# Dividing attention by its sums on GpSimd, in the layout in which it is summed

## The chip, the cores and the metric

The kernel runs on one core of a Trainium2 chip, as one launch. The metric is the time on the device in microseconds, the median of several runs. The engines are called by their short names: PE (TensorE: matmuls, with PEld for its weight loads), DVE (VectorE), ACT (ScalarE), POOL (GpSimd) and SP (SyncE, which here issues DMAs).

## The reference

One conformer block over 2 x 4000 tokens of 144 features, 4 heads of 36, in bfloat16:

```
h = silu(layernorm(x) @ w_ff1a) @ w_ff1b;      x = x + 0.5 * h
q, k, v = split(layernorm(x) @ w_qkv)          # 4 heads of 36
p = softmax(q @ k.T * 36 ** -0.5);             x = x + (p @ v) @ w_o
a, b = split(layernorm(x) @ w_pw1)
c = depthwise_conv5(a * sigmoid(b), dw);       x = x + silu(c) @ w_pw2
h = silu(layernorm(x) @ w_ff2a) @ w_ff2b;      x = x + 0.5 * h
out = layernorm(x)
```

Attention is over all 4000 keys of a sequence, for each of its 4000 queries.

## The kernel before

**Tiles.** The 8000 tokens are 16 chunks of 500 (`CH`), eight to a sequence; a chunk is 4 blocks of 125 tokens. For a chunk of queries attention runs over 62 tiles of 64 keys and a rest of 32, 1008 tiles in all. A tile's scores for the four heads are four 64x64 matmuls, in two banks of PSUM with 128 rows (two heads) by 1000 columns. Then comes the exponential, by one of the ways in the table `TYPES`:

- 'A': ACT does it in one instruction (PT<-PS, 128x1000); 'R' is the same for the rest.
- 'D': DVE does it in five: two passes from PSUM to integers (one for each bank, 128x500), then on the tile in SBUF "y" and "w" (TENSOR_SCALAR on 16-bit integers, 128x1000) and "m" (TENSOR_TENSOR). 'W' is the same with one pass over both banks (128x1000). The sums of these tiles take twice the matmuls.

Four or eight matmuls (PS<-PT,VA) add the tile to two PSUM banks `BX` and `BX+1`: by column, the 500 queries; by row, 36 features of one head and, in row 36, the sum of the exponentials; from row 64 on, the next head. This is the column layout: features down the partitions, tokens along the columns.

**The end of a chunk.** `epilogue` copies the two banks to SBUF as f32 (`OTF`, 128x1000, laid over columns of the queries QT that are no longer read; DVE COPY QT<-PS). PE transposes it, eight f32 matmuls against an identity (PS<-IDF,QT), into two banks with tokens down the partitions. There the sum is a column: for each bank DVE takes the reciprocal (RD<-PS) and multiplies (AN<-PS,RD, 125x288). `post1` transposes the result AN back with one DMA on SP (XTB<-AN); only the last chunk does it with PE. The output projection is eight matmuls of 72 rows (PS<-WO,XTB), added to x by `residual`. Then the chunk's layer norm, GLU, convolution and second feed-forward follow.

**Layer norms.** DVE takes statistics, POOL a power and the normalisation XN<-X,RS, block by block, and a DMA on SP transposes XN. Some of these, and copies and residual additions, can be done by another engine; a letter for each in the table `UNITS` says which ('d' DVE, 'a' ACT, 'p' POOL). A residual on ACT adds x on PE, with two further matmuls against EYE or IDENT.

**Order.** A planner in Python (`Rec`, `Sched`) writes down the instructions with costs and dependences. The tables then fix what runs: `ORDER` the order on each engine, `TYPES` the exponentials, `BANKS` and `SLOTS` the places of the attention tiles, `PLACES` other banks, `UNITS` the engines. Each engine runs its list in order, with waits on semaphores only where a dependence needs one. The first chunks' feed-forward and projections come ahead of any exponential; afterwards the other work of the block runs between the tiles; after the last exponential the tail holds what is left of the last chunks. All instructions are issued from one helper (L588 to L595), so groups in the profile are told apart by tiles and shapes.

Of the kernel before, what the change touches and what calls it, by code (L numbers as in the profile page):

```python
# [13 lines left out]
H = 4  # L14
# [26 lines left out]
        '+9+&+##.+[+Z+T+O+E+_+`+R+S+J+I+K+2+8+U+c+d+k+3+H+h+g+6+7+N+r+q#/+v+u+l+i+b+^+f+z+y+a,&+]+}+j,!+s+t+w'
        '+X,++e+x,%#0,1,0+{+Y,*,$+o+p,4,5#1,8,9+V#2,=,<,),2+m+W,G,#,7,F,A,@+n,:,3,6,K,J,(+|,>,;,/,,,N,O,H,S,I'
        ',.,R,-,?,Z#3,W,V,L,Q,M,P,b,a#4,f,e,[,X,U,T,Y,i,j#5,m,n,d,B,q,C,x,w#6,{,|,g,l,c,r-#-$#7-)-(,h,k,z-,,p'
        '-2-3,o#8-6-7,y-+-*,E-%-&-;-:,}-!,^,_,]---?->#9-C-B,u-K-<-9-=-8-F-G-4,`,D-1-P-Q,t-.,v-@-5-J-U-T-D-E-X'
        '-I-0-/-_-`-Y-A-H,s-d-c#<-g-h#:#;#>#?#=-k-l-o-b-p-e-f-w-j-N-W-i-V-O-t-s#@#A#B-x-a.!-}#C.&.%-L-S-R-M.*'
        '.+./-q-r.#-u-v...$#D#E.8.9-^.-.,.).<.=-]#F.@.A.;.3.:-m-n.D.E.0#G.1-{.I.H.2-z.>.?.(.L.M-|.P.Q-Z.K.B.^'
        '._-y.O.F-[.T.C.N.J.G.b.c.7.R.S.X.f.6.5.g.j.V.U.4.k.W#H#I.a.h.u.t.`.y.x.e.d.n.|.}#J.o.l.m.z/%.i/$.{/)'
        '/-/#.[/*.Z/!.v.].Y.w/4/3#K/7/8/./+/,/(/</;#L/@/?#M/I/C/J.p/6/5/:/9/N/M.s.q/A/D.r/&/B#N/Q/R/L///U/P/_'
        '/=/V/K#O/Z/Y/2/^/1/>#P/d/m/n/O/0/W/F/[/H/r/q#Q/u/v/h/E/G/c/]/g0$0#/T/S/a/b/`/X0(0)/y/f/e0302#R07060,'
        '0%0;/s0:0&04/p/o050+0-0E0D0*/t/z/w09080H0I0=0</x0>/k0L0M0F/l#S0P0Q#T0U0T/j/i0G0?/}0Y0X0K0N#U0d0c0!0R'  # L50
        '0]0S0J0g0h/|0l/{0Z0[0k0O#V0o0p000/0j0i010e0s0t0.0^0f0V0w0x#X#W0{0W0|0B0C0m1#0v0n0y1$0u#Y1.1/0q0z1!1('
        '0}0b1213#Z161710111)0r0a1:1;#[1>1?#]1B1C1%0A#^1&1J0@1A1G1F1P1Q151<0`181K0_1@191U1T#_#`1I1R1Y1D1X1W1H'
        '1]1M1O1V1^1L1*1S1a1-1N1g1h1b1=141l1k#a1v1u1o1[1,1+1z1y#b2!1}1p1e1i1x1E2-2,2%1`1{1|1_21202$1w1Z1f2#2&'
        '2425#c2>232?1m1j282C2/2B1n1c1q1d#d2F29222G1s1r2Q2P2E2*2+2@262K2A2D2J2U2T2)2.2H1t2X2Y2I#e2(2^2W2]2b2['
        '2a2;2:#f272e2`2S2l2f2<2V2m2N#g2i2r3#2R2s2g2=2w2L2v2M2_2Z2h2c2O3!2d2{2z2k2j3)3*#i3-3.#j2p2q3132#h3536'
        '2y3+3/2x3:393B3A302n342|3=3>372}332o3G383H#k3K3L3,3S3?3%2u3O3P3$3;3T2t3@3I3Z3Y3F3N3M3&3<3_3^3f#l3J3C'
        '3c3[3b3g3m3l3(3Q3a3D3`3R3x3W3X3p3q#m3u3t3]3d3E4(3e3n3j3o3r4#3V4!3U3s4&473y#n#o4-4.3h3i4$3k4%414B4A3v'
        '483w4>4=#p#q#r4I4J4E4F4D4)424/4?40#s4+4,4M4N#t#u4Q4@4C4R4G4L4H4;4V4U4*4O#w#v4a4`3}4K4P494Y4e4d4:#x4h'
        '4i4<3|4T4S4Z4W4s4r454X4m4f4g3z4w4v4l4643444b3{4{4z#y#z5#4t5!5-4u4j5.4}4y4[4x4k4c4|5&52515(4]5$4q4p55'
        '56#{5=5%595:4_4o4^5D5C5>5350574n545/5X5W5<5G5+585N5M#|5F5`5;5H5Q5,5Y5Z5[5]5E5B5O5*5a5)#}5A5P5d5e5^5_'  # L60
        '5?5R5@5i5h$!5m5l$#5q5p5t5f5g6!5}5j5J5b5c5k5I5w6&6%5L5r5o5s5K5x5n5V5U6*6+5T5S5u5v$$6/6.6962$%686(636<'
        '6=$&$(6A6@6$6#6)$)6:6E6?6D656I666;6H$*61606S6R6,6C6L675z6B6W6V$+646M6F5|6Z6G6>6[6e6Y6U5{6f6X6_6-6T6K'
        '$,$-6j6i6^6m6g6]6n6N6O6J6h5y6`6P6w6x$.6q6p6{6Q6o6|6k6l6y6r7#7$$/7(7)$0$17-7,6}6b706d767!7%77$26a717&'
        '7.7;7:6v6u7>7E6z787/7D$37H7I7*7?797<7+6c7M7L$47Q7P7G7F6s6t7T7U$5$674757X7Y7]7S$77d7c7C7J7B7^7g7K7V7h'
        '7R7O7N737q7=7k7r$87v7u7f7i7j727e7l7z7y$97@7W8(8)7}7A7s7b7Z7[8,8-$:81807t7w8!7_7`8*8584$;8?8>83827p88'
        '7|7a8+8B8C7{$<8.8/8F8G8@89867x$=878J8K8D8A7o8&8N8E8H8U8T$>8X8Y7m8$8%8O8L8M8]8^$?8#8W7n8V8g8h8;8a8:8['
        '8Z8I8k8l$@8p8o8`8i8R8b8P8j8s8t$A8x8w8r8q$B8{9)9*8u8=8n9-8Q8<8y9.9!8v8S8m8|8}92918c8d8e8f8_8z96959#$C'
        '9?9@909/9C9D9,99$D9H9G94939:97989+9R9Q$E9F9&9U9V9B9E9K9(9Z9Y$F9_9^9S9L9J9A9$9c9b9%9I9f9]9T9[9l9m$G9p'
        '9q9=9e$H9t9u9X9W9g9`9a9d:#9O:!9>9;9<9r9x9o:(:&$I:,9M9y:$9N:+9P9n:5:6:/:%9j9s9k:::99v:0:.$J:=:*:>:-:B'
        ':)9h:A9}$K:L:E:K9z9{:?:8:7:@:4:O:C:P:3:F9i:<:;:T:S:M:D9w:W:^:_$L:2:X:b:c:U:R:V:G:a:f:N:g:1:H:`:j9|:q'  # L70
        ':p$M:k:I:u:t:d:J:[:e:s:|:i:x:y:r:];&;($N$O;-;.:Y:Z:}:Q;2;1$P;<;;:m:h:{;?;0:n:l;@;/;3:o;4;C;D;5:v;=$Q'
        ';*:z;M;N:w;A;+;B;R;G;Q;%;E;6;$;V;U;);F;H;>;Z;Y$R$S;P;,;W;^;X;_;[;b;O;S;c;7;T$T;];8;f;m;9;#;l;I;L;!;J'
        ';q;K;p;g;e;d$U;t;u;`;o;s;n;x;y$V;|;};r;a<)<$<%$W<,;k;j<-;z;:<7<6;{<2<3;v$X$Y<A<@<*<+<;<:<D<E<#<!;h<('
        '<&;w<H<I;i$Z<M<L$[$]$^$_$`<P<Q<T<C<4<U<?<8<5<B<K<J<N<O<0<9<X<Y<.<1<></<G<]<a<^$a<g<h<S<Z<b<V<F<[<l<k'
        '$b<`<_<v<u<W<o$c<y<z<n<m<R<j<p<<=!<}$d=%=&$e<c<d=*=+<w<{<|=$=2=/=.=)=#<i=3<x=8=9=(=-$f=<==<==L$g=A=@'
        '$h$i$j=E=:=D=?=;=6=1=>=5=4=I<s=M=H<e=7<t<f=,=S=R=B=c=G=F=C=V=W$k=[=Z<q=d=U=J=K=T=_=`$l=i=j=X=Y=^=y<r'
        '=0=m=n$m=q=r=]=z=Q=P=k=l=u=v$n>$>#=s=t=N=O>)>($p$o>,>-=a=}=h>%>1>:>&>0=f=x=w=b=e>7>6=g=p>A>*>/>@$q=o'
        '>!>E>D>;$r>H>I>C=|>B={>+>M>L$t>.>9>P>Q$s>[>Z$u>`>_>U>N>4>5>8>S>c>d>T>K>?>R>J>3>g>h$w$v>l>F>k>G>^>o>='
        '>]>u>v>>>b>a>j>e>f>O>z>y$x>p>m>}><?!>x>i>2>|?&>w>W?%>n>X$y$z?#?2?*?+?(>{?$${?.>Y?7$|?8>s?>?=?,?-?)?1'
        '>r>V?A?B>q>t?0?/?F?E?I?P?O?T?C?D?S$}?W?X?J?6?5?@???V?G?c?b?[?R?Q?g?f%!?Y?k?j?H?d?]?U?<?9?:?;?e?n?Z?t'  # L80
        '?u%#%$?x?y?l?m?o?|?}?h%%@$@%%&?w?z@*?v@)?{@-?i@3?a@4@&%(?M@.?`?N@8@7?3@,@<@+?4@!@A@B@;@#@6?_@5@E@F?^'
# [2417 lines left out]
```

## Time and profile before

| what | value |
|---|---|
| time, median of 3 runs | 868.47 us (868.26 to 868.83) |
| span of the profiled execution | 866.2 us, 27018 instructions |
| granted TensorE clock, mean | 0.999 |
| busy: PE, DVE, ACT, POOL | 98%, 96%, 96%, 33% of the span |
| exponentials on ACT | 777, mean 1080 ns |
| f32 transposes on PE | 128, in groups of four |
| DMA | 26.92 MB, mean 31 GB/s |

The page shows one execution. It gives that execution's span, from the first to the last instruction, and no other time of it; the runs' median is 2.3 us above the span. Busy time counts an engine while at least one of its instructions is under way, and successive instructions overlap at their ends, so durations of a group add up to more than the engine's busy time.

### The profile page before, as it was taken

To read this page: it belongs to the slowest core of one execution; us is meant where nothing else is said; L and a number is where in the kernel's file an instruction comes from. 1 tells how busy PE (TensorE), PEld (TensorE's weight loads), DVE (VectorE), ACT (ScalarE), POOL (GpSimd) and SP (SyncE) were. 2 spreads that over 40 slices of the span, in tenths; PEclk is the share of its full clock that TensorE was granted. 3 is DMA by queue.
4 is the path that set the end of the run, shared out by engine and by line. 5 is a ranking of instruction groups with operands and counts; after the bars stand their busy time and mean duration, and the time that the engine had idled before them with its cause. 6 is when DMAs were issued, how large, how long until landed. Compare 5 with 4: busy or idle time off the path is not lost.

```text
span 866.2 us, 27018 instructions
## 1 busy us (share of the span) xinstructions
PE 849.7 (98%) x11585; PEld 412.0 (48%) x11585; DVE 835.1 (96%) x1819; ACT 834.9 (96%) x1096; POOL 283.2 (33%) x562
## 2 busy tenths in 40 slices
PE   9999999999999999999999999999999999999996
PEld 8644434444344444444444444445444444445585
DVE  7999999999999999999999999999999999999986
ACT  6999999999999999999999999999999999999975
POOL 7771331041334301441230060320550173300854
PEclk9999999999999999999999999999999999999999
DMA  3331111102113110211210020110130021100121
GB/s 102 83 54 21 33 21 38 21 14 45 34 26 51 17 24 2 51 27 39 33 39 2 2 44 3 21 26 14 26 49 4 12 48 39 26 2 14 41 47 50
DMA packets 86331, 26.92 MB, mean 31 GB/s; under 512 B 81384, under 2 KB 86210, under 8 KB 86210
## 3 DMA queue, kind: packets, MB, share of 16 engines
q1 hardware_dynamic: 84662, 24.34, 15.0%
q8 instruction: 91, 1.49, 0.7%
q10 hardware_dynamic: 1548, 0.84, 0.4%
q14 instruction: 30, 0.25, 0.1%
HBM read 3.31 MB, written 2.30 MB: 6 GB/s over the span
## 4 chain that ended last, share of the span: by engine, by line
ACT 40%; PE 40%; DVE 17%; DMA 1%; issue 0%; POOL 0%; DVEq 0%; ACTq 0%
PE PS L589 40%; ACT PT L589 37%; DVE PT L589 12%; ACT TH L589 3%; DVE ST L589 1%; DVE QT L589 1%; DVE HT L589 1%; DVE U L589 1%; DVE X L589 1%; DMA X<-in_x_dram 0%; DMA out_dram<-XN 0%; DVE XN L589 0%; DVE KT L589 0%; ACT X L589 0%; DVE AN L589 0%
## 5 line engine op out<-in xcount | busy, mean ns | idle before, releaser
L589 ACT ACTIVATE PT<-PS 128x1000 bf16<-128x1000 f32 (+1 forms) x793 | 730.0, 1072 | 4.9 <-PE PS L589 4.1
L589 PE MATMUL PS<-QT,KT 64*64 64x500 bf16 x3968 | 460.2, 383 | 4.2 <-ACT PT L589 1.2
L589 PE MATMUL PS<-PT,VA 64*37 64x500 bf16 x4828 | 449.6, 372 | 1.3 <-DVE QT L589 0.5
L589 DVE TENSOR_SCALAR PT<-PS 128x500 int16<-128x500 f32 x425 | 279.8, 678 | 4.3 <-PE PS L589 2.9
L589 PEld LDWEIGHTS PS<-QT,KT 64*64 64x64 bf16 x3968 | 139.8, 104 | 201.9 <-ACT PT L589 99.9
L589 PEld LDWEIGHTS PS<-PT,VA 64*37 64x37 bf16 x4828 | 163.1, 96 | 105.5 <-issue 16.2
L589 POOL TENSOR_SCALAR RS<-ST 125x4 f32<-125x4 f32 (+1 forms) x132 | 31.0, 237 | 479.9 <-DVE ST L589 476.0
L589 DVE TENSOR_SCALAR PT<-PT 128x1000 uint16<-128x1000 uint16 x430 | 172.6, 419 | 1.8 <-DVE PT L589 0.2
L589 DVE TENSOR_TENSOR PT<-PT 128x1000 bf16<-128x1000 bf16 x215 | 144.9, 678 | 0.8
L589 POOL TENSOR_SCALAR XN<-X,RS 125x144 bf16<-125x144 bf16 x250 | 142.4, 581 | 3.9 <-POOL RS L589 0.5
L589 POOL TENSOR_TENSOR RS<-RS,NHALF 125x4 f32<-125x4 f32 (+2 forms) x93 | 92.0, 993 | 50.7 <-DVE RS L589 48.6
L589 ACT ACTIVATE TH<-PS 128x500 bf16<-128x500 f32 (+3 forms) x175 | 92.8, 560 | 3.5 <-PE PS L589 3.0
L589 DVE SCALAR_TENSOR_TENSOR HT<-TH,PS 128x500 bf16<-128x500 bf16 (+1 forms) x120 | 71.5, 616 | 0.8 <-ACT TH L589 0.5
L589 PE MATMUL PS<-XTB,WA 72*128 72x500 bf16 (+2 forms) x280 | 71.3, 359 | 0.6 <-DVE PT L589 0.2
L589 DVE BATCH_NORM_STATS2 ST<-X 125x6 f32<-125x288 bf16 (+1 forms) x160 | 65.6, 449 | 1.9 <-DMA X<-in_x_dram 1.2
L589 DVE SCALAR_TENSOR_TENSOR X<-PS,X 125x288 bf16<-125x288 f32 x114 | 50.8, 451 | 6.7 <-PE PS L589 5.6
L589 PE MATMUL PS<-WB,HT 128*125 128x144 bf16 (+1 forms) x640 | 52.2, 229 | 0.1
L589 PEld LDWEIGHTS PS<-WB,HT 128*125 128x125 bf16 (+1 forms) x640 | 44.9, 136 | 13.4 <-issue 3.9
L589 PEld LDWEIGHTS PS<-XTB,WA 72*128 72x128 bf16 x280 | 21.5, 97 | 28.9 <-issue 8.3
L589 PE MATMUL PS<-U,DG 128*128 128x375 bf16 (+7 forms) x204 | 28.0, 263 | 0.1
L589 POOL COPY U<-U 128x2 bf16<-128x2 bf16 (+1 forms) x54 | 10.6, 229 | 42.5 <-DVE U L589 32.3
L589 ACT ACTIVATE HT<-PS 128x500 bf16<-128x500 f32 (+3 forms) x43 | 20.6, 537 | 3.4 <-PE PS L589 2.9
(95 smaller groups left out, 522.1 us busy)
## 6 DMA issues: line engine op xcount, KB each, us to landing
X<-in_x_dram SPq DMA_DIRECT2D x16, 140.6 KB
XTQ<-XTB SPq DMA_DIRECT2D x24, 70.3 KB
out_dram<-XN SPq DMA_DIRECT2D x12, 140.6 KB
XTB<-XN SPq DMA_TRANSPOSE x53, 3.6
out_dram<-XN ACTq DMA_DIRECT2D x2, 140.6 KB
XTB<-AN SPq DMA_TRANSPOSE x15, 3.2
WA<-in_w_ff1a_dram ACTq DMA_DIRECT2D x1, 144.0 KB
WB<-in_w_ff1b_dram ACTq DMA_DIRECT2D x1, 144.0 KB, 2.6
```

The costliest lines, as they stand in the source:

```text
L589: ins = getattr(eng, o.name)(*o.a, **o.k)
```

## The change

For 15 of the 16 chunks `epilogue` no longer transposes. The planner still places the old instructions ("ghosts", so that the rest of its plan stays), and `drop` removes them. In their place, behind the copy to `OTF`:

```diff
+    def att(c):
+        return dead(c)[:, :, 0:CH]
+
+    def reciprocals(c, OTF, k0):
+        op("sp", "dma_start", sums[c], OTF[DH:DH + 65:64, :, :], q="r0", ...)
+        op("sp", "dma_start", RL[0:100, 0, :], sums[c].rearrange("h z (a n) -> (h z a) n", n=20), q="r3", ...)
+        op("dve", "reciprocal", RL[0:100, 1, :], RL[0:100, 0, :], r=["RL"], w=["RR"], cost=0.1)
+        op("sp", "dma_start", recips[c].rearrange("h (a n) -> (h a) n", n=20), RL[0:100, 1, :], q="r1", ...)
+        n = DH if c else 64
+        for h in range(2):
+            op("sp", "dma_start", RB[64 * h:64 * h + n, :, :].rearrange("p z n -> p (z n)"),
+               recips[c, h:h + 1, :].to_broadcast([n, 2 * CH]), q=f"r{4 + h}", r=[("RC", c)], ...)
+        a = (att(c), OTF, RB[:, :, :])
+        k = dict(op=ALU.mult)
+        R.unit([op("pool", "tensor_tensor", *a, **k, r=[("RB", 0), ("RB", 1), "OTF"], w=k0, cost=MUL)], "p",
+               {"d": [("dve", "tensor_tensor", a, k, c_dve(2 * CH), None)]})
...
-                c, g, lambda i: [(xt1(s1, k, i), WO[0:HD, k, :]) for k in range(2)], 1.0,
+                c, g, lambda i: [((att(c) if c < NCH - 1 else XT[:, s1])[:, k, i * TB:(i + 1) * TB], WO[:, k, :]) for k in range(2)], 1.0,
...
-            z0 = (c - 1 - (c == NQR)) % NQR * CH
-            OTF = QT[:, :, z0:z0 + 2 * CH].bitcast(F32)
+            z0 = (NQR - 8 if c == NQR else (c - 1) % NQR) * CH
+            return QT[:, :, z0:z0 + 2 * CH]
...
-            if zz:
-                otf_done.add(c)
+            otf_done.add(c)
```

The sums (rows 36 and 100 of `OTF`) go by DMA to DRAM, come back as 100x20, DVE takes one reciprocal, and they go to DRAM again; two DMAs spread them over the 36 rows of each head (64 for the first chunk) into `RB` (128x1000 f32). One instruction multiplies `OTF` by `RB` into bfloat16 (`att`, in the same columns of QT). The output projection takes its weights from there, over 128 rows; `WO` is loaded in that layout by two DMAs, with zeros between the heads. The columns of QT stay in use until the projection. The last chunk keeps its transposes, with 128 rows in the second. Planner costs of the new steps are `MUL` = 2.3, `LAT_R` = 2.0 and `LAT_B` = 4.0.

A second new piece joins y, m and w of two DVE tiles into single instructions over 2000 columns, for the 13 pairs in a new table:

```diff
+PAIRS = (
+    (102, 107), (393, 400), (528, 533), (543, 546), (606, 610), (630, 635), (702, 707), (722, 727),
+    (764, 770), (775, 778), (787, 790), (833, 838), (967, 968),
+)
```

All order tables are new. `TYPES` has 778 'A', 213 'D', 1 'W' and 16 'R' (before 777, 210, 5 and 16). `UNITS` has 15 more letters, for the multiplies, all 'p'. Laid over the old table, 'a' falls from 57 to 32: eight residuals fewer on ACT, four pairs of normalisations, and the rest copies (nine of transposes, one of K and two of Q, of 500 columns each, and one of 72).

More of the change, by code (lines that the diff above doesn't have):

```diff
@@ L41 @@
[L41 to L45, printed above, removed]
@@ L405, in op, with aside, drop, ghost @@
         self.ops.append(o)
+        return o
+    def aside(self, make):
+        was = dict(self.free), self.last, self.issue, list(self.quad), self.kind
+        n = len(self.ops)
+        self.step += 1
+        make()
+        self.step += 1
+        self.free, self.last, self.issue, self.quad, self.kind = was
+        for o in self.ops[n:]:
+            o.t0, o.t1, o.done = o.t0 - 1e4, o.t1 - 1e4, o.done - 1e4
+    def drop(self):
+        gone = self.ghosts
+        self.ops = [o for o in self.ops if id(o) not in gone]
+        for o in self.ops:
+            o.deps = [d for d in o.deps if id(d[0]) not in gone]
+            o.shared, o.own = o.shared - gone, o.own - gone
+    def ghost(self, *a, **k):
+        o = self.op(*a, **k)
+        self.kept.append(o)
+        self.ghosts.add(id(o))
         return o
@@ L1083, in bass_standalone__conformer_family_zipformer__speech_kernel @@
     lanes = [0]
-    load("sp", "w2", WO[0:HD, :, :], kh(w_o), ["WO"])
+    R.ghost("sp", "dma_start", None, None, q="w2", w=["WO"], cost=0.45)
     load("sp", "w2", WP1[0:HD, :, :], kh(w_pw1), ["WP1"])
@@ L1919, in epilogue @@
     def epilogue(c, part):
-        if c:
-            z0 = (c - 1 - (c == NQR)) % NQR * CH
-            OTF = QT[:, :, z0:z0 + 2 * CH].bitcast(F32)
-        else:
-            OTF = QT[:, 0, (NQR - 4) * CH:NQR * CH].bitcast(F32).rearrange("p (z n) -> p z n", z=2)
-        k0 = ["OTF0"] * (c == 0) + [("OT", c)]
+        OTF = otf(c)
+        put = op if c == NCH - 1 else R.ghost
+        k0 = ["OTF0"] * (c == 0) + [("OT", c)] + [("OT", NQR - 7 + i) for i in range(2) if c == NQR]
         ps, rk = PSV[:, BX:BX + 2, 0:CH], [("ps", BX), ("ps", BX + 1)]
@@ L1942, in epilogue @@
                                      c_act(2 * CH), None)]})
+        if c < NCH - 1:
+            R.aside(lambda: reciprocals(c, OTF, k0))
         a = yield need("dve", anp)
@@ L2209, in settle @@
                         readers[n, hh, bk[hh]] = zs
-                deps, last = [(z, True) for z in zs], None
-                chain = {}
-                for i, what in enumerate("ymw"):
-                    name, a, k = ymw_args(what, *sl)
-                    more = [] if last is None else [(last, True if what == "m" else False)]
-                    chain[what] = last = fresh("dve", name, a, k, COST[what], "e", deps + more, (n, what), 2 + i)
-                chain["w"].deps.append((chain["y"], False))
-                made = {0: (zs, [chain["w"]]), 1: ([chain["y"]], [chain["m"]])}
+                made = zs
+            parts.append((n, ph, rest, kind, sl, made))
+        chains = {}
+        for n, ph, rest, kind, sl, zs in parts:
+            if kind not in "DW" or n in led:
+                continue
+            m = lead.get(n)
+            wide = () if m is None else tuple(parts[m][4])
+            zs = zs if m is None else zs + parts[m][5]
+            deps, last = [(z, True) for z in zs], None
+            chain = {}
+            for i, what in enumerate("ymw"):
+                name, a, k = ymw_args(what, *sl, *wide)
+                more = [] if last is None else [(last, True if what == "m" else False)]
+                chain[what] = last = fresh("dve", name, a, k, COST[what + "2" if wide else what], "e", deps + more,
+                                           (n, what), 2 + i)
+            chain["w"].deps.append((chain["y"], False))
+            chains[n] = chain
+            if m is not None:
+                chains[m] = chain
+        for n, ph, rest, kind, sl, made in parts:
+            if kind in "DW":
+                chain = chains[n]
+                made = {0: (made, [chain["w"]]), 1: ([chain["y"]], [chain["m"]])}
             v_deps = [(d, raw) for d, raw in outside(old[n, "O"]) if raw]
```

547 lines of the change are left out of this document (299 added, 248 removed).

## The prediction

> **What bounds the kernel now.** I read the page's busy times first, then three stretches of the span, then the chain that ended last, and then who waits for whom.
>
> ```profile
> PE 849.7 (98%) x11585; PEld 412.0 (48%) x11585; DVE 835.1 (96%) x1819; ACT 834.9 (96%) x1096; POOL 283.2 (33%) x562
> 0.00:60.00 60.00, 58.40 (x725) 39.52 (x725) 53.61 (x146) 50.53 (x91) 47.59 (x104) 1.00 0.36 81
> 60.00:820.00 760.00, 753.01 (x10441) 341.53 (x10444) 747.28 (x1560) 753.41 (x937) 213.55 (x419) 1.00 0.14 26
> 820.00:866.20 46.20, 38.26 (x429) 30.92 (x428) 34.16 (x116) 30.92 (x69) 22.10 (x41) 0.97 0.22 50
> ACT 40%; PE 40%; DVE 17%; DMA 1%; issue 0%; POOL 0%; DVEq 0%; ACTq 0%
> PEld PS L589 <- ACT PT L589: 109.1, 341, 0.8
> PEld PS L589 <- DVE PT L589: 72.2, 237, 0.6
> ```
>
> The columns of the stretch rows are PE, PEld, DVE, ACT, POOL, clock, DMA share and GB/s. From 60 to 820 us three engines are full at once: PE 753, ACT 753, DVE 747 of 760 us. The ends are looser (ACT 50.5 of 60 and 30.9 of 46.2). The chain says the same: ACT 40%, PE 40%, DVE 17%, so no single engine owns the time, and it jumps between them. The two wait rows (inside that stretch) show how they hold each other: PE's weight loads stand 109 us for ACT's exponentials and 72 us for DVE's, short waits of at most 0.8 us, partly covered by matmuls still running.
>
> Busy hides some slack, since neighbouring instructions overlap:
>
> ```profile
> 130.56 5.65 ACT L589 ACTIVATE PT<-PS 128x1000 bf16<-128x1000 f32 x6
> 135.91 0.78 ACT L589 ACTIVATE TH<-PS 128x500 bf16<-128x500 f32 x1
> 131.74 0.67 DVE L589 TENSOR_SCALAR PT<-PS 128x500 int16<-128x500 f32 x1
> 132.33 0.67 DVE L589 TENSOR_TENSOR PT<-PT 128x1000 bf16<-128x1000 bf16 x1
> 132.92 0.20 DVE L589 RECIPROCAL RD<-PS 125x8 f32<-125x8 f32 x1
> 133.16 0.46 DVE L589 TENSOR_TENSOR AN<-PS,RD 125x288 bf16<-125x288 f32 x1
> 133.53 0.41 DVE L589 TENSOR_SCALAR PT<-PT 128x1000 uint16<-128x1000 uint16 x1
> L589 ACT ACTIVATE PT<-PS 128x1000 bf16<-128x1000 f32 x777 | 723.1, 1080 | 4.9 <-PE PS L589 4.1
> ```
>
> Six exponentials fill 135.91 - 130.56 = 5.35 us, 0.89 each, against a mean duration of 1.08. An ACT wait below 0.19 us therefore shows as no idle time. A DVE instruction takes about 0.08 us less of the engine than its duration (131.74 to 132.33 is 0.59 for a duration of 0.67). I cost DVE and ACT work by such spacings.
>
> **The change, part by part.** The rows for what goes and what moves:
>
> ```profile
> L589 PE MATMUL PS<-IDF,QT 128*125 128x128 f32 x128 | 22.3, 297 | 0.0
> 132.11 0.70 PE L589 MATMUL PS<-IDF,QT 128*125 128x128 f32 x4
> 132.74 0.41 PE L589 MATMUL PS<-QT,KT 64*64 64x500 bf16 x4
> L589 DVE TENSOR_TENSOR AN<-PS,RD 125x288 bf16<-125x288 f32 x32 | 14.5, 454 | 0.4
> L589 DVE RECIPROCAL RD<-PS 125x8 f32<-125x8 f32 x32 | 6.5, 203 | 0.3
> L589 PE MATMUL PS<-WO,XTB 72*125 72x144 bf16 x128 | 14.1, 236 | 0.0
> L589 PE MATMUL PS<-WP,SW 128*125 128x144 bf16 x62 | 11.7, 241 | 0.1
> L589 DVE SCALAR_TENSOR_TENSOR X<-PS,X 125x288 bf16<-125x288 f32 x112 | 49.8, 451 | 4.6 <-PE PS L589 3.6
> L589 ACT ACTIVATE X<-PS 125x288 bf16<-125x288 f32 x14 | 6.2, 443 | 1.4 <-PE PS L589 1.4
> L589 PE MATMUL PS<-X,EYE 125*125 125x144 bf16 x24 | 3.5, 225 | 0.0
> L589 DVE TENSOR_SCALAR PT<-PS 128x1000 int16<-128x1000 f32 x5 | 6.0, 1196 | 0.1
> L589 DVE TENSOR_SCALAR PT<-PS 128x500 int16<-128x500 f32 x420 | 273.8, 672 | 4.3 <-PE PS L589 2.9
> ```
>
> PE: 15 of 16 chunks lose their 8 f32 transposes. Four of them hold PE from 132.11 to 132.74, 0.63 us, so 30 such groups are 18.9 us. The output projection keeps its 8 matmuls per chunk, now over 128 rows in place of 72; the 128-row WP row has 241 ns beside 236 for WO, so nothing is added. Eight residual additions fewer run on ACT (14 codes 'a' before, 6 after), each with two EYE matmuls: at the 0.7 us that eight WO matmuls take together (row at 742.61 below) 16 are 1.4 us (at most 16 x 0.225 = 3.6). PE loses 20 us.
>
> DVE: 30 pairs of reciprocal and product go. A pair fills 132.92 to 133.53 = 0.61 us, and 0.49 without the wait between its two: I take 0.55, or 16.5 us. Added are 15 reciprocals of 100x20, bounded by the 8-column reciprocal (0.20) and a 500-column pass (0.67), near the former: 15 x 0.2 = 3 us. The 13 joined pairs of tiles save 39 instructions' fixed part. That part is 1.196 - (1.196 - 0.672) x 2 = 0.15 us by durations and 0.07 after the overlap, so 39 x 0.07 = 2.7. The tile table has one DVE tile fewer (214 against 215; one exponential more on ACT): a tile is 2 x 0.59 + 2 x 0.33 + 0.6 = 2.4 us. Back to DVE come 8 residuals (x 0.37 = 3.0) and three copies of Q or K (x 0.59 = 1.8). Sum between 60 and 820 us: -16.5 + 3 - 2.7 - 2.4 + 3 + 1.8 = -13.8 us.
>
> ACT in that stretch: minus 8 x 0.35 and 3 x 0.5, plus one exponential of 0.89: -3.4 us. Most of what else leaves ACT (nine transpose copies, four pairs of normalisations) leaves in the ends, where ACT isn't the bound; I give it nothing, and a microsecond either way if it shortens or lengthens the last stores.
>
> GpSimd: 15 multiplies of 128x1000 f32, off the path of everything but their own chunk's projection. The rows nearest:
>
> ```profile
> L589 POOL MEMSET XN<- 128x1024 bf16 x5 | 4.7, 947 | 0.0
> L589 POOL MEMSET NHALF<- 128x4 f32 x1 | 0.1, 101 | 0.0
> L589 POOL TENSOR_SCALAR XN<-X,RS x250: 452/461/1742, 16.2 to 856.4; 125x144 bf16<-125x144 bf16 x125
> L589 DVE TENSOR_SCALAR PT<-PT x430: 366/414/687, 56.8 to 819.3; 128x1000 uint16<-128x1000 uint16 x144
> L589 DVE TENSOR_SCALAR XN<-X,ST,RS x62: 291/312/1054, 6.8 to 861.6; 125x144 bf16<-125x144 bf16 x60, 126x144 bf16<-126x144 bf16 x2
> ```
>
> A memset of the size takes 0.95 us; the normalisation, which reads and computes, takes 0.46 for 144 columns, at most 0.46 / 144 x 1000 = 3.2 us for 1000. I take its slope without a start cost, (0.461 - 0.101) / 144 = 2.5 ns, so 2.5 us and 38 us in all. POOL, at 214 of 760 us, has room. The Trainium skill (GPSIMD Engine Reference, 3.1 Elementwise) measured 4497 ns for a two-input f32 pass of 2048 columns; an estimate from it is 2.2 us here, and 33 us in all, which POOL would hold as well.
>
> But the last two rows also show a price on DVE. The same instruction that normally takes 0.414 us once took 0.687, and DVE's normalisation 1.054 in place of 0.312, while POOL's reached 1.742: the two engines hold each other up. 430 of these PT instructions in some 760 us are one every 1.8 us, so a 2.5 us multiply meets one. Its price is between nothing and about 2 us of DVE each; the longest hold-up shown is 0.27 for PT and 0.74 for XN, and I take 1.0, 15 us in all. It counts on the path with DVE's share of the chain.
>
> The new chain: DVE's copy of the sums, then a DMA out, one back, the reciprocal, one out, two spreads, the multiply.
>
> ```profile
> 727.64 1.20 DVE L589 COPY QT<-PS 128x1000 f32<-128x1000 f32 x1 [0.16 <-PE PS L589]
> 742.61 0.71 PE L589 MATMUL PS<-WO,XTB 72*125 72x144 bf16 x8
> X<-X SPq DMA_DIRECT2D x1, 0.6 KB, 2.0
> WB<-in_w_ff1b_dram ACTq DMA_DIRECT2D x1, 144.0 KB, 2.6
> XTB<-AN SPq DMA_TRANSPOSE x15, 3.2
> ```
>
> Three small DMAs at 2.0, a spread of 144 KB per half at 2.6 (twice that at worst), the copy 1.2 and the multiply 2.5 make 1.2 + 6 + 0.2 + 2.6 + 2.5 = 12.5 us, or 15 at the worst. In the trace of before the projection came 15.0 us behind the copy (727.64 to 742.61) where it came soonest, so the chain mostly fits even where the projection stays in its place, and I cost it at nothing. If a searched order put the projection closer, PE, which takes its work in order, would stand with scores and sums behind it, and ACT after it. On SP, five DMAs replace one transpose per chunk; each waits for the one before, and XN's transposes stand behind them. That costs nothing as long as those are needed later than the wait of some 2 us; otherwise the same stall of PE.
>
> **The sum.** Relief counts by the chain's share of each engine: PE 20 x 0.40 = 8.0, DVE 13.8 x 0.17 = 2.3, ACT 3.4 x 0.40 = 1.4, less the hold-ups 15 x 0.17 = 2.6. That is 9.1 us off the span of 866.2, so 857.1. The page gives no other time of that execution; the median of the runs, 868.5, lies 2.3 us above its span. So I forecast 859.4, rounded to **860**.
>
> **The rivals.** First, the shares could be too small: if PE is what ACT waits for wherever it waits, most of PE's 20 us comes through and the time is 868.5 - 18 = 850. Against it: ACT's exponentials alone need 777 x 0.89 = 692 us, and its 753 of 760 us leave little to win by waiting less.
>
> Second, ACT holds the time. Its own work falls by 3.4 us only, and freed PE and DVE then wait for it: 865.
>
> Third, slower: the multiplies shut DVE out. If each costs the full 2 us, DVE gains 13.8 and loses 30, and if PE, which is held up by DVE's tiles 237 times already, hands all of it on, the time is 868.5 - 11.7 + 30 = 887; half of it gives 872. It decides from about 11.7 / 15 = 0.8 us handed on per multiply. For it: the maxima above. Against: 250 POOL normalisations are in the trace of before, and the median PT instruction did not move. A rule of the skill's speaks for this rival: the Trainium skill (SBUF — State Buffer, Who interferes with whom) says that DVE and GpSimd share one pair of ports as an exclusive lock, held for the whole instruction, against DVE instructions with two SBUF inputs or in a two-port mode. By that rule the hold-up would be the whole remainder of each multiply, the 2 us end; the trace agrees on the hold-ups (0.27 and 0.74 us) but has no POOL read longer than those to show the size.
>
> Fourth, slower too: the chain comes late. Landings of 3.5 us in place of 2.0 make it some 18 us, and where orders leave 15, PE stands 1 us per chunk or more: 860 + 15 = 875. For it: five dependent waits on one queue; against: the 15.0 us gap is the tightest.
>
> That the change isn't made is no case: all 15 new codes in the table of choices are 'p', GpSimd.
>
> **How the numbers follow.** Forecast 860 (855 to 866) 0.42; PE's relief comes through (850) 0.14; ACT holds (865) 0.11; hold-ups 0.20 and late chain 0.13, of which 0.07 together end near 868.5. Within 0.2% is 1.7 us, about what a measurement of this kernel can tell from no change. So faster 0.67, same 0.07, slower 0.26. The range takes in 850 below and 876 above: 0.05 lies under it and 0.12 over it.
>
> **What would show it.** Right: the f32 matmuls down from 128 to 8, PE's busy time between 60 and 820 us down with the stretch, DVE's products on AN down from 32 to 2, the chain's PE share below 40%, ACT's share above. Wrong: PT instructions on DVE with a mean well above 0.42 us beside POOL multiplies (third), PE waits for a DMA or for POOL ahead of the WO matmuls (fourth), multiplies beyond 3.2 us, or ACT with as much idle and waiting as before although PE has less to do (the order, not the load, sets the time).

## The result, and the profile after

The changed kernel takes **894.91 us** (median of 4 runs, 891.79 to 900.57) against 868.37 us (868.11 to 868.83) on the same chip: a ratio of 1.0315, 95% interval 1.0297 to 1.0332. It is slower by 3.1%. The prediction said 860 us, with a range of 850 to 876, so it was wrong, in sign too. The profiled execution took 893.93 us, its span 892.1.

These are the rows of after that answer to those of before: the page's busy times and the chain's shares, then the three stretches (columns as there), then who waited for whom (over the whole span).

```profile
PE 856.3 (96%) x11445; PEld 396.2 (44%) x11445; DVE 840.3 (94%) x1750; ACT 828.0 (93%) x1068; POOL 330.6 (37%) x586
...
PE 40%; DVE 28%; ACT 23%; DMA 4%; POOL 3%; issue 1%; ACTq 0%; DVEq 0%; SPq 0%; POOLq 0%
```
```profile
0.00:60.00 60.00, 56.16 (x575) 38.60 (x575) 47.25 (x132) 39.61 (x75) 37.29 (x86) 0.89 0.33 69
60.00:820.00 760.00, 735.81 (x10078) 313.89 (x10076) 732.13 (x1453) 737.32 (x906) 247.75 (x410) 1.00 0.14 27
820.00:892.10 72.10, 64.32 (x804) 43.75 (x794) 60.91 (x167) 51.06 (x90) 45.60 (x90) 0.97 0.18 42
```
```profile
PEld PS L618 <- DVE PT L618: 88.8, 252, 1.9
ACT PT L618 <- PE PS L618: 20.4, 33, 2.6
PEld PS L618 <- DMA XTB<-XN: 8.3, 7, 2.4
PE PS L618 <- DMA XTB<-XN: 5.8, 4, 2.1
```

What the change takes away is gone: 140 matmuls and 69 DVE instructions fewer. But from 60 to 820 us PE, DVE and ACT are each 15 to 17 us less busy than before, in the same 760 us. That is not slack won. The wait rows show that all of them stand now. The longest wait of PE's loads for DVE's PT was 0.6 us and is 1.9; ACT waits 20.4 us for PE, where it was 4.1; and PE's loads wait 8.3 us for XTB<-XN (a transposed layer norm), where it was 0.6. In the chain DVE went from 17% to 28% and ACT from 40% to 23%.

I measured the loss along the kernel by the start of the same score matmul (PS<-QT,KT, the k-th of 3968) in both traces. After is 9.2 us behind at 55 us already, and 26.1 behind at the last score; the tail from there is as long as before (47.5 and 47.7 us). Between, the loss comes in steps of 1 to 3 us with flat stretches. Where after catches up at all, it is by at most 2.2 us and not for long, so the relief isn't seen at any place.

**The first step, at the front.** SP's own queue in the timeline, first of before, then of after with one row of PE (start, duration, instructions, and in brackets the idle time before and what ended it); then windows of after.

```profile
22.66 10.84 SPq L589 DMA_TRANSPOSE XTB<-XN  x3
33.55 4.79 SPq L589 DMA_DIRECT2D X<-in_x_dram  x8
```
```profile
23.12 1.34 SPq L618 DMA_TRANSPOSE XTB<-XN  x1
24.51 5.05 SPq L618 DMA_DIRECT2D X<-in_x_dram  x8
30.32 6.39 SPq L618 DMA_TRANSPOSE XTB<-XN  x2
37.82 1.01 PE L618 MATMUL PS<-XTB,WA 72*128 72x500 bf16 x2 [2.11 <-DMA XTB<-XN]
```
```profile
36.00:37.00 1.00, 0.00 (x0) 0.00 (x0) 0.58 (x2) 0.18 (x1) 0.25 (x2) 1.00 0.67 130
38.00:39.00 1.00, 1.00 (x6) 0.56 (x5) 0.00 (x0) 0.13 (x1) 0.91 (x2) 0.50 0.10 19
50.00:51.00 1.00, 1.00 (x10) 0.63 (x9) 0.58 (x3) 0.00 (x0) 0.83 (x2) 0.50 0.00 0
52.00:53.00 1.00, 1.00 (x13) 0.74 (x11) 0.15 (x1) 1.00 (x3) 0.23 (x1) 1.00 0.06 16
```

The new order issues the second sequence's eight loads of X (1.1 MB, needed much later) behind the first transpose of XN, where the old one had them behind the third. The two transposes behind them are late, and the PE row says the rest: 2.11 us of standing for XTB<-XN. The last four rows are the windows, of 1 us each, with the granted clock in the third column from the right. After the stand the clock is 0.50 from 38 to 51 us, though PE is busy all the time. Half a clock for 13 us is 6.5 us of work; with the stand that makes 8.6 of the 9.2 us. The Trainium skill (TensorE: Matmul & The Clock Gate, Why this matters for your kernels) warns of idle gaps over some 3 us; the trace has the drop after 2.1 us, so a shorter one is enough here. The Trainium skill (TensorE: Matmul & The Clock Gate, Part 1: The HAM clock gate) has the full clock back after at least one busy window of some 3.4 us; here it took 13 us of busy PE.

**The steps in the middle.** One of the 15 multiplies, on POOL, with DVE beside it and PE after it:

```profile
293.89 2.30 POOL L618 TENSOR_TENSOR QT<-QT,RB 128x1000 bf16<-128x1000 f32 x1 [4.77 <-DMA RB<-recips]
293.63 0.67 DVE L618 TENSOR_SCALAR PT<-PS 128x500 int16<-128x500 f32 x1
294.21 0.22 DVE L618 CAST VA<-PS 128x72 bf16<-128x72 f32 x1
294.35 2.38 DVE L618 TENSOR_TENSOR PT<-PT 128x1000 bf16<-128x1000 bf16 x1
297.38 0.61 PE L618 MATMUL PS<-QT,KT 64*64 64x500 bf16 x6 [1.46 <-DVE PT L618]
```

DVE's pass "m" usually takes 0.67 us. Here it takes 2.38, to 296.73, and the multiply ends at 296.19: m did its work only when POOL was done. PE then stands 1.46 us for it. While a multiply runs, DVE instructions that read PSUM, such as the two before m, have their usual time; the first y, m or w, which go from SBUF to SBUF, waits. Nine of the 15 multiplies held one, for 0.23 to 2.11 us beyond the usual time of its shape and 11.1 us in all (in the trace of a_front below ten, 11.4 us); in the other six DVE was at other work. The Trainium skill (SBUF — State Buffer, Who interferes with whom) has this rule, and here the trace agrees: held to the end of the instruction.

```profile
L618 POOL TENSOR_TENSOR QT<-QT,RB 128x1000 bf16<-128x1000 f32 x15 | 33.3, 2218 | 92.6 <-DMA RB<-recips 92.6
L618 DVE TENSOR_SCALAR PT<-PT 128x1000 uint16<-128x1000 uint16 x376 | 156.1, 432 | 3.2 <-PE PS L618 1.7
L618 PE MATMUL PS<-WO,QT 128*125 128x144 bf16 x120 | 13.2, 237 | 0.2 <-POOL QT L618 0.2
```

The multiplies take 2218 ns each, where 2.5 us was forecast. The mean of y and w over 1000 columns is 432 ns, where that of before was 419: the few held ones hardly show in it. The projection from `att` waits 0.2 us for POOL in all: the chain of sums, DMAs and multiply is not late for it. POOL's 92.6 us of waiting for RB cost nothing.

**The late transposes.** A third kind of step has neither load nor multiply near it:

```profile
309.65 2.11 POOL L618 TENSOR_TENSOR RS<-RS,NHALF 125x4 f32<-125x4 f32 x2 [1.95 <-DVE RS L618]
312.36 4.94 POOL L618 TENSOR_SCALAR XN<-X,RS 125x144 bf16<-125x144 bf16 x8
317.32 2.70 SPq L618 DMA_TRANSPOSE XTB<-XN  x2
322.17 0.60 PE L618 MATMUL PS<-XTB,WA 72*128 72x500 bf16 x2 [1.59 <-DMA XTB<-XN]
```

Power, eight normalisations and transposes follow each other without room, and PE has the feed-forward's first matmuls (XTB,WA) in its list 1.59 us too early for them. There are such stands at 726 and 736 us too (0.75 and 1.31 us).

### The profile page after: what moved, and what is told of

Read it like the earlier page. It is cut to its first block, busy times and chain, and to the rows that moved or that the text cites. A ratio compares the mean times of both kernels' runs of the same rounds, so it can differ in the third digit from the quotient of the medians.

```text
span 892.1 us, 26734 instructions
## 1 busy us (share of the span) xinstructions
PE 856.3 (96%) x11445; PEld 396.2 (44%) x11445; DVE 840.3 (94%) x1750; ACT 828.0 (93%) x1068; POOL 330.6 (37%) x586
## 3 DMA queue, kind: packets, MB, share of 16 engines
q8 instruction: 89, 1.46, 0.7%
## 4 chain that ended last, share of the span: by engine, by line
PE 40%; DVE 28%; ACT 23%; DMA 4%; POOL 3%; issue 1%; ACTq 0%; DVEq 0%; SPq 0%; POOLq 0%
PE PS L618 40%; ACT PT L618 21%; DVE PT L618 19%; DMA XTB<-XN 2%; DVE ST L618 2%; ACT TH L618 2%; POOL XN L618 2%; DVE X L618 1%; DVE XN L618 1%; POOL RS L618 1%; DVE HT L618 1%; DVE U L618 1%; DMA out_dram<-XN 1%; DMA X<-in_x_dram 0%; DVE KT L618 0%
## 5 line engine op out<-in xcount | busy, mean ns | idle before, releaser
L618 ACT ACTIVATE PT<-PS 128x1000 bf16<-128x1000 f32 (+1 forms) x794 | 732.0, 1061 | 21.9 <-PE PS L618 20.4
L618 PE MATMUL PS<-QT,KT 64*64 64x500 bf16 x3968 | 457.3, 385 | 14.1 <-ACT PT L618 3.4
L618 PE MATMUL PS<-PT,VA 64*37 64x500 bf16 x4824 | 462.4, 374 | 4.2 <-DVE PT L618 3.0
L618 POOL TENSOR_SCALAR RS<-ST 125x4 f32<-125x4 f32 (+1 forms) x137 | 37.6, 276 | 384.0 <-DVE ST L618 378.4
L618 DVE TENSOR_SCALAR PT<-PT 128x1000 uint16<-128x1000 uint16 (+1 forms) x402 | 175.5, 453 | 3.5 <-PE PS L618 1.7
L618 POOL TENSOR_SCALAR XN<-X,RS 125x144 bf16<-125x144 bf16 x256 | 148.5, 592 | 4.3 <-POOL RS L618 0.5
L618 DVE TENSOR_TENSOR PT<-PT 128x1000 bf16<-128x1000 bf16 (+1 forms) x201 | 146.8, 733 | 1.4
L618 PE MATMUL PS<-XTB,WA 72*128 72x500 bf16 (+2 forms) x280 | 74.0, 372 | 4.8 <-DMA XTB<-XN 4.5
L618 POOL TENSOR_TENSOR QT<-QT,RB 128x1000 bf16<-128x1000 f32 x15 | 33.3, 2218 | 92.6 <-DMA RB<-recips 92.6
L618 DVE SCALAR_TENSOR_TENSOR X<-PS,X 125x288 bf16<-125x288 f32 x122 | 54.1, 450 | 11.0 <-PE PS L618 10.5
L618 PEld LDWEIGHTS PS<-WB,HT 128*125 128x125 bf16 (+1 forms) x640 | 47.1, 142 | 12.8 <-issue 4.2
L618 ACT ACTIVATE HT<-PS 128x500 bf16<-128x500 f32 (+3 forms) x43 | 20.3, 538 | 12.9 <-PE PS L618 12.4
```

What stands on the lines that cost most here:

```text
L618: ins = getattr(eng, o.name)(*o.a, **o.k)
```

## The experiments

My theory from the trace: the loads at the front cost about 9 us, the multiplies' hold on DVE about as much, late transposes the rest; and the relief is worth little, because ACT and DVE are still full. The rivals: DVE's load itself (multiplies cost what DVE lacks, wherever they run), the DMA chain on SP, and the new order as a whole.

**The front.** In the changed kernel the eight X loads go back behind the third transpose (a_front); in the kernel before they go behind the first (b_front). Both are one edit of SP's list, with the index 2 or 0:

```diff
+            if e == "sp":
+                late = [o for o in lines[e] if o.q in {f"x{c}" for c in range(8, 16)}]
+                lines[e] = [o for o in lines[e] if o not in late]
+                i = [j for j, o in enumerate(lines[e]) if o.name == "dma_start_transpose"][2]
+                lines[e][i + 1:i + 1] = late
```

> The changed kernel with one edit: on SP the eight loads of the second sequence's X go behind the first three transposes of XN, as in the kernel before, where the new order puts them behind the first one. Theory (the transposes queue behind 1.1 MB of loads, PE stands 2.1 us at 35.7 us and then has half its clock until about 52 us): the scores that are 9.2 us late at 55 us are at most 1 us late, no half clock between 35 and 55 us, time 894.9 - 9 = 886. Rival (the first 60 us are longer because nine copies and a pair of normalisations moved from ACT to DVE): the granted clock returns but 5 us or more of the 9.2 stay, time 890 to 895.

> The kernel before with one edit: on SP the eight loads of the second sequence's X go ahead, behind the first transpose of XN, as the new order has them. Theory: the same loss without any of the change, 868.4 + 9 = 877, with half the clock somewhere between 35 and 55 us. Rival (it takes the new order on the other engines too): 868 to 870.

Measured: a_front 884.76 us, ratio 1.0195 (1.0177 to 1.0212); b_front 875.62, 1.0081 (1.0053 to 1.0109). Moving these loads explains 10 of the 26.5 us, and the same move costs the old kernel 7.5. One of the four executions of b_front had a mean clock of 0.998, as before has, and took 871.38 us, 3.3 over before; the other three, at 0.990 to 0.991, took 875.57 to 877.66. By that execution most of this loss is the clock behind the stand. The trace of b_front has the same picture, stand, clock and all:

```profile
37.97 1.02 PE L594 MATMUL PS<-XTB,WA 72*128 72x500 bf16 x2 [2.51 <-DMA XTB<-XN]
```
```profile
40.00:45.00 5.00, 5.00 (x22) 2.68 (x21) 2.59 (x6) 2.24 (x4) 2.16 (x6) 0.50 0.00 0
```

**The multiplies in pieces, narrowed, and on DVE.** a_split cuts each multiply into four of 250 columns, a_front_split does so with the loads put back, a_front_split8 has eight of 125:

```diff
+        cuts, ops = [(z, n, n + CH // 2) for n in (0, CH // 2) for z in range(2)], []
+        for z, n0, n1 in cuts:
+            a = (att(c)[:, z, n0:n1], OTF[:, z, n0:n1], RB[:, z, n0:n1])
+            ops.append(op("pool", "tensor_tensor", *a, op=ALU.mult, ...))
```

> The changed kernel with each multiply on POOL cut into four instructions of 250 columns; nothing else. Theory (one multiply holds DVE off SBUF for its whole length, PE stands behind DVE and after two of these stands loses clock): hold-ups on DVE fall from 11 us to some 3, none over 0.7 us, PE's stands of 1.3 to 1.5 us at five multiplies go, time 894.9 - 8 = 887. Rival (those losses come from the searched order, with PE too close behind DVE's tiles, and the multiply is only nearby): 893 to 896, with the stands still there.

> Both edits, loads behind the transposes and multiplies in four. If the two losses are separate: 894.9 - 9 - 8 = 878, still slower than before, since PE's and DVE's relief shows nowhere and some transposes of XN still come late. If they overlap (the same slack is used twice): 883 to 886.

> The changed kernel with the X loads put back and each multiply in eight pieces of 125 columns of one half (one piece: 884.8, four pieces: 879.3, a tenth of the columns: 873.0). Nothing is left out. If an instruction of DVE is held for at most what is left of one piece: holds of at most 0.3 to 0.4 us, which ACT and TensorE mostly don't see, 875 to 877. If the price goes by the multiply's time as a whole, whatever its pieces: 879 to 880, as with four.

Measured: a_split 887.02 us, 1.0227 (1.0182 to 1.0272); a_front_split 879.29, 1.0128 (1.0111 to 1.0145); a_front_split8 879.90, 1.0134 (1.0119 to 1.0150). Four pieces give back 5.5 to 8 us; eight give no more, against my 875 to 877. The groups of one piece (a_front), of four and of eight, and the timeline of a_front_split8 at two projections show why:

```profile
L623 POOL TENSOR_TENSOR QT<-QT,RB 128x1000 bf16<-128x1000 f32 x15 | 33.3, 2219 | 89.3 <-DMA RB<-recips 89.3
```
```profile
L623 POOL TENSOR_TENSOR QT<-QT,RB 128x250 bf16<-128x250 f32 x60 | 45.3, 785 | 91.3 <-DMA RB<-recips 91.3
```
```profile
L623 POOL TENSOR_TENSOR QT<-QT,RB 128x125 bf16<-128x125 f32 x120 | 56.8, 510 | 92.2 <-DMA RB<-recips 92.2
```
```profile
630.13 0.71 PE L623 MATMUL PS<-WO,QT 128*125 128x144 bf16 x8 [1.03 <-POOL QT L623]
706.95 0.46 PE L623 MATMUL PS<-WO,QT 128*125 128x144 bf16 x4 [1.19 <-POOL QT L623]
```

A piece costs more than its share (510 ns for an eighth of 2219), so the multiply of a chunk ends later, and now it is late for the projection: PE stands 1.03 and 1.19 us for POOL, where it was 0.61 us with four pieces and 0.18 with the whole multiply. Each hold got shorter, at most 0.53 us with four pieces and 0.26 with eight. Counting those over 0.15 us, they add up to 11.4 us with one piece, 10.6 with four and 6.7 with eight. So with four pieces nearly the same sum of holds costs half as much, and by the trace of eight a new wait took the place of what was won; no run takes that wait away.

a_front_nomul leaves the division out: the multiplies take 100 of 1000 columns, and the projection reads IDENT. a_front_dve moves the whole multiplies to DVE at the places where they ran in the trace of a_front:

```diff
-        a = (att(c), OTF, RB[:, :, :])
+        a = (att(c)[:, :, 0:50], OTF[:, :, 0:50], RB[:, :, 0:50])
...
+        for o in self.muls:
+            lines["pool"].remove(o)
+            o.eng = "dve"
```

> The changed kernel with the eight X loads behind the third transpose (884.8 before this), and the multiplies narrowed to 100 of 1000 columns; the projection takes the identity as its weights in place of the product, so the division of 15 chunks is left out. DMAs, reciprocals and order are kept. If the multiplies' hold on DVE is the price: the stands behind multiplies go, 1.26 + 1.49 + 1.46 + 0.71 + 1.15 + 1.43 = 7.5 us and the low clock behind two of them, some 2 us: 875 to 877. If the DMA chain or the new order is the price: 883 to 885.

> The changed kernel with the loads behind the transposes and all 15 multiplies on DVE, each at the place in DVE's order at which POOL began it. DVE has 15 x 1.1 = 16.5 us more, and no POOL multiply holds it up. Theory (the loss is the hold-up, in which DVE stands for up to 2.1 us and PE behind it; DVE has slack for the work itself): 884.8 - 7 = 878, no stand of PE over 1 us at a multiply. Rival (DVE is full, its own work costs as much as the hold-ups): 885 to 892.

Measured: a_front_nomul 872.97 us, 1.0059 (1.0042 to 1.0076); a_front_dve 887.08, 1.0228 (1.0213 to 1.0243). Without their length the multiplies' price is gone, all 11.8 us of it (884.76 to 872.97), more than the 8 to 10 I had expected. Low clock is not the price: the two executions of a_front with a mean clock of 0.998 and 0.999 took 885.23 and 884.30 us, the three of a_front_nomul with 0.997 to 0.998 took 872.03 to 873.12. The projection waits for no multiply in a_front_nomul, but in a_front that was 0.18 us in all. On DVE the multiplies take 15 x 1193 ns, 17.9 us, and the kernel is 14.1 us over a_front_nomul. It is no faster than with POOL's, where my theory had 878:

```profile
L631 DVE TENSOR_TENSOR QT<-QT,RB 128x1000 bf16<-128x1000 f32 x15 | 17.9, 1193 | 0.1
```

By the score matmuls a_front_dve was 6 us ahead of a_front at 290 us and 1.2 us behind at the end. So for this division both engines' ways are a cost to DVE: by occupying it, or by holding it.

**What is left.** a_front_free leaves out the five DMAs and the reciprocal of each chunk too. a_front_near is that kernel with 444 matmuls of the feed-forwards and the GLU reading a constant tile, so that PE waits for no XN transpose from about 100 us on:

```diff
+        gone = {id(o) for e in ("sp", "dve") for o in lines[e] if o.name == "reciprocal" and o.a[0].shape[0] == 100
+                or o.q in ("r0", "r1", "r3") or o.q in ("r4", "r5") and o.a[0].tensor.name == "RB"}
...
+            if o.name == "matmul" and o.k["rhs"].tensor.name == "XTB" and any(d[0].name == "dma_start_transpose" for d in o.deps):
...
+                o.deps = [d for d in o.deps if d[0].name != "dma_start_transpose"]
```

> As the run before, and also without the five DMAs and the reciprocal of each of the 15 chunks (the division left out wholly): all that the change relieves, none of what it adds. If the added steps are the whole price and the relief is worth what the prediction said: 868.1 - 9 = 859. If the relief is worth nothing and the added steps cost the rest: 868. If the newly searched order itself is slower than the old one: 872 or more, near the run before.

> The changed kernel with the X loads put back, without multiplies, DMAs and reciprocals (875.3 before this), and with 444 matmuls of the feed-forwards and the GLU (WA, WE, WP, WPZ, from about 100 us on) reading a constant tile in place of the transposed XN; the transposes still run. So TensorE waits for no transpose of XN there; the division and what those matmuls read are left out. If late transposes are what the new order costs: the stands of 1.36, 1.47 and 1.47 us go, 875.3 - 4.3 = 871, and with the smaller delays behind them 868 to 870. If the new order is slower for another reason: 874 to 876.

Measured: a_front_free 875.33 us, 1.0078 (1.0063 to 1.0094), within the intervals as a_front_nomul: the DMAs and reciprocals cost nothing that shows. (Its trace has two stretches of 3.4 us at half clock behind stands for XTB<-XN; that of a_front_nomul has none ahead of the tail.) It is not at 868, nor at the 859 that the prediction's relief would give, though none of the added steps is left but a tenth of each multiply. a_front_near: 869.79 us, 1.0022 (1.0012 to 1.0031). The waits, first of a_front_free, then of a_front_near (for a DMA or POOL; the 1.5 us for NHALF stand in all these kernels, that of before too):

```profile
PEld PS L631 <- DMA XTB<-XN: 6.4, 5, 1.9
PE PS L631 <- DMA XTB<-XN: 4.3, 3, 1.5
```
```profile
PE PS L641 <- POOL NHALF L641: 1.5, 1, 1.5
```

So late transposes of XN in the new order take 3 to 5.5 us (from a_front_nomul or from a_front_free to a_front_near), the low clock behind their stands included, and they are late without any DMA of the division on SP's queue. What is left to make them late is the new order.

**The relief alone, in the old order.** Cuts in the kernel before, each leaving part of the work out: b_pe does one f32 transpose of each four; b_act takes the exponentials over 488 of 500 columns; b_dve the passes y, m and w over 940 of 1000; b_pe_act and b_all combine them.

```diff
+                if i and c < NCH - 1:
+                    cuts.add(id(o))
...
-        return (PT[:, pt, :, :], PSV[:, lo:hi + 1:hi - lo, 0:CH], ACT.Exp), k
+        return (PT[:, pt, :, 0:CH - 12], PSV[:, lo:hi + 1:hi - lo, 0:CH - 12], ACT.Exp), k
...
-        zu, yu = (PTU[:, q, :, :].rearrange("p b n -> p (b n)") for q in (z, y))
+        zu, yu = (PTU[:, q, :, :].rearrange("p b n -> p (b n)")[:, 0:940] for q in (z, y))
```

> The kernel before, with one f32 transpose in place of four in each of the 30 groups (three of every four blocks of the attention output are left out; DVE reads the one block four times, at the same cost). PE has 30 x 0.47 = 14 us less, nothing else changes. The prediction's step (relief counts by PE's 40% of the chain): 868.1 - 5.6 = 862.5. Rival (PE's relief shows nowhere while the order stays and ACT has its full work): 867.5 to 868.5.

> The kernel before, with ACT's 777 exponentials over 488 of 500 columns in each half (the last 12 columns are left out; the tiles' rest stays as cleared). ACT has 777 x 24 x 0.82 ns = 15 us less, nothing else changes. By the prediction's shares (ACT 40%): 868.1 - 6.1 = 862. Rival (ACT sets the pace of the middle, and each of its microseconds is one of the kernel's): 868.1 - 13 = 855.

> The kernel before, with y, m and w of DVE's 215 tiles over 940 of 1000 columns (the last 60 are left out). DVE has 215 x 0.063 = 13.6 us less, as much as the change takes from it. By the prediction's shares (DVE 17%): 868.1 - 2.3 = 866. Rival (DVE has slack, its relief shows nowhere): 868.

> The kernel before with both cuts at once: one transpose in place of four per group in 15 chunks (TensorE 14 us less, alone worth 0) and exponentials over 488 of 500 columns on ACT (15 us less, alone -5.2 us). Left out: three of four transposes, and the exponentials of 12 columns. If TensorE's relief is worth its share of the chain (0.40) once ACT is relieved too: 868.1 - 5.2 - 5.6 = 857.3. If the engines wait for each other in the written order and TensorE only follows: 862.6, the ACT cut alone.

> As the run before, and DVE's y, m and w over 940 of 1000 columns as well (13.6 us less, alone -1.7). If the three gains only add as measured one by one: 868.1 - 0 - 5.2 - 1.7 = 861.2. If the three engines bind jointly, so that TensorE's 14 us counts only once both others are lighter: most of the smallest of the three cuts, 13 us, so 855. Left out: as named, and the last 60 columns of those DVE passes.

| cut | median us | ratio (95% interval) | gain us |
|---|---|---|---|
| PE, 9.8 us | 868.22 | 1.0006 (0.9996 to 1.0016) | 0 |
| ACT, 15 us | 862.60 | 0.9941 (0.9926 to 0.9955) | 5.2 |
| DVE, 12.9 us | 866.18 | 0.9979 (0.9970 to 0.9989) | 1.7 |
| PE and ACT | 862.34 | 0.9935 (0.9920 to 0.9949) | 6.0 |
| all three | 856.73 | 0.9868 (0.9851 to 0.9884) | 11.6 |

The sizes of the cuts are those of the traces, by the busy time of the groups that were cut: the f32 transposes fall from 22.3 to 12.5 us (14 were expected, at 0.47 a group), the exponentials from 723.1 to 708.1, y, m and w from 317.5 to 304.6.

PE's relief shows nothing alone and nothing beside ACT's that is clear of the intervals. The trace of b_pe shows where it goes. These are the transposes and the scores behind them; the prediction shows the same two rows of before, at 132.11 and 132.74:

```profile
131.88 0.37 PE L589 MATMUL PS<-IDF,QT 128*125 128x128 f32 x1
132.44 0.41 PE L589 MATMUL PS<-QT,KT 64*64 64x500 bf16 x4 [0.19 <-ACT PT L589]
```

The scores follow 0.56 us behind the one transpose, where it was 0.63 behind four: PE now stands for ACT's exponential instead. PE's busy time falls by 5.1 us (849.7 to 844.6) and its idle time grows by 5.0, of which 4.3 stands right behind the transposes, in 24 of the 30 groups.

All three cuts together gain 11.6 us, well over the 6.9 of the single gains. Whether PE's cut has a part in that isn't shown: ACT's and DVE's cuts without PE's were not run together, and 11.6 is more than PE's 9.8. The page's chain of the kernel with all three cut, and of the one without ACT's 12 columns:

```profile
PE 55%; ACT 32%; DVE 9%; POOL 2%; DMA 1%; issue 1%; DVEq 0%; POOLq 0%; ACTq 0%
```
```profile
PE 61%; DVE 22%; ACT 15%; DMA 1%; issue 1%; POOL 0%; DVEq 0%; ACTq 0%
```

The share of the engine that was cut falls (ACT from 40% to 15% with its own cut), and another takes its place. In the kernel before, each engine's relief alone comes through by about a third or less, and the three cuts together give nearly as much as DVE's is large (12.9 us).

## Why the prediction was wrong

**The account.** By the ratios the 3.15% are: the X loads 1.20% (10.4 us; 7.5 in the old order), the multiplies 1.36% (11.8), late transposes 0.37% to 0.56% (3.2 to 4.9), and 0.22% (1.9) remains with all of that taken out. A gain from the relief shows in none of these kernels.

**The term for PE failed first.** 20 us x 0.40 = 8.0 us was most of the forecast gain. The cut of three quarters of the same transposes measured 0, where by that term its 9.8 us would give 3.9. PE's share of the chain says where the chain ran, not what a lighter PE gives: with ACT and DVE full, PE stands for ACT's exponential in the time that was freed. The first rival (PE comes through, 850) falls with it. The second, ACT holds the time, was right that a freed PE waits for ACT and that ACT's own relief is small; I gave it 0.11. But ACT does not hold the time alone: its cut of 15 us gave 5.2, not 13. The terms for the other two engines held where they could be tried: ACT's 0.40 gave 5.2 for 15 us (0.35), DVE's 0.17 gave 1.7 for 12.9 (0.13).

**The holds were sized well, and their weight was wrong.** I took 15 us of holds and counted 0.17 of them, 2.6 us. The trace of a_front has 11.4 us of holds, and the multiplies cost 11.8: nearly all of it comes through, a factor of 1, not 0.17. Why is argued, not shown: a cut is spread over hundreds of instructions and is lost in other waits, while a hold of 2 us comes at once, and PE and ACT have little to cover it (ACT's slack was 0.19 us per exponential by the prediction's own reading). That four pieces, with 10.6 us of holds of at most 0.53, cost 6.3 us (879.29 less 872.97) agrees. The third rival stated this mechanism, and 11.8 / 15 = 0.79 us per multiply was measured. That this is the 0.8 at which the prediction's sum would have come out even is chance: the relief in that sum did not come. The rule of the Trainium skill (SBUF — State Buffer, Who interferes with whom) that I set beside it was the better guide than the median PT instruction beside normalisations, which I named as evidence against. In the trace of before, 97 of y, m and w began while a normalisation ran on POOL, and none took over 0.28 us longer; the size of a hold by a multiply could not be read there.

**The order was costed at nothing.** The prediction followed the steps that the diff moves in the code, and not the transfers that new order tables move. It costed SP's queue for the five DMAs (right: nothing) and never asked where the X loads stand to the transposes of XN, or where XN's normalisations stand to PE. These are 14 to 15 us, with the clock the larger part of the front's. The 13 joined pairs of tiles are part of that order too, and were not tried by themselves. That "all order tables are new" stood in the text ahead of it; it needed a term of its own, with a stand and the clock behind it as the price.

**What held.** The multiply's 2.5 us (2.22), its chain in time for the projection (0.2 us of waiting), the f32 matmuls down to 8 and DVE's products on AN down to 2, and the tail the same within a microsecond (47.5 and 47.7 us). Of the signs named as right, PE's share below 40% and ACT's above did not appear (40% and 23%). Of those named as wrong, ACT waiting more although PE has less to do did. The mean of PT instructions hardly moved (0.432 us for 0.419 in y and w); the hold shows in the longest of them, 2.52 us.

**What stays open.** The 1.9 us that a_front_near is over the kernel before, and why not even the 3 us or so that DVE's and ACT's relief should give by the measured weights are seen in it. PE still stands 5.6 us there in nine places over 0.3 us (1.3 in three before), the longest 1.49 us at 106 us ahead of WQKV,XTQ; whether that is all was not tried. What ACT's and DVE's cuts give together without PE's was not tried either.

## What to carry to other kernels

Where several engines are full together, a chain's share isn't a price for relief: PE had 40% of the chain and its relief gave 0, while cuts on all three gave more together (11.6 us) than one by one (6.9). An added stall is another matter: 15 long holds cost here nearly what they measure (11.8 us for 11.4). So weigh a saving spread over many instructions and one long block on a shared path by different factors. When an order is searched anew, read the new queues for what passes ahead of what: eight loads moved by two places cost nearly as much as the multiplies did.

## What the hardware showed

- A stand of 2.1 us brought the granted clock to 0.50, and it stayed there for 13 us of busy PE; the same in the old kernel after 2.5 us. A stand of 1.49 us at 201.9 us was followed by 3.4 us at 0.50, and so were two of 0.63 and 0.52 us close together (at 478.6 and 480.7 us), while single stands of 1.59, 1.46 and 1.43 us (at 321, 296 and 589 us) were not followed by a lower clock. So the length of one stand does not decide it in these traces. Ahead of the tail the stretches at 0.50 lasted 13.7, 3.4 and 3.4 us in after, 13.7 in b_front and 20.5 at the front of a_split, all multiples of 3.4. The rows are windows of after.

```profile
202.00:203.00 1.00, 0.00 (x0) 0.00 (x0) 1.00 (x3) 0.61 (x2) 0.14 (x1) 1.00 0.00 0
206.00:207.00 1.00, 1.00 (x12) 0.33 (x8) 0.61 (x1) 1.00 (x2) 0.00 (x0) 0.50 0.00 0
298.00:300.00 2.00, 2.00 (x56) 1.11 (x52) 2.00 (x5) 2.00 (x3) 0.00 (x0) 1.00 0.03 8
482.00:484.00 2.00, 2.00 (x18) 0.63 (x11) 1.97 (x5) 0.91 (x1) 0.00 (x0) 0.50 0.00 0
```

- POOL's product of two f32 tiles has a fixed part: 2219 ns for 1000 columns, 785 for 250, 510 for 125, by estimate from these 0.2 to 0.3 us each. The same product over 1000 columns took 1193 ns on DVE.
- Not everything that runs on POOL holds DVE's y, m and w. The multiply held them to its end (2.38 us in place of 0.67). In the trace of before some began with up to 1.25 us of a POOL normalisation still to run and were no longer than usual; why isn't shown.
